# Attention: earlier places for the odd head's score tiles, and other places for values, maxima and decoding

## The chip, the cores and the metric

The kernel runs on one core of a Trainium2 chip. A core has TensorE (PE in the profile; its weight loads are shown apart as PEld), VectorE (DVE), ScalarE (ACT), GpSimd (POOL) and SyncE (SP, which issues most transfers). The metric is device time of one execution in microseconds. Three runs of the kernel before gave 985.89 us in the median, 984.61 at the lowest and 988.9 at the highest.

## The reference, cut to what matters

Attention with a threshold on each row of scores, and then two feed-forward layers on its output. The change touches the attention alone: 4 batches of 8 heads, 576 positions, 64 columns a head.

```python
scale = 1.0 / np.sqrt(q.shape[-1])
scores = scale * np.matmul(q, k.transpose(0, 1, 3, 2))
thresh = np.max(scores, axis=-1, keepdims=True) - tau
scores = np.where(scores >= thresh, scores, -1000000000.0)
scores = scores - np.max(scores, axis=-1, keepdims=True)
attn = np.exp(scores)
attn = attn / (np.sum(attn, axis=-1, keepdims=True) + 1e-09)
return np.matmul(attn, v).astype(np.float32)
```

The weights of the two layers arrive as 64-bit floats; the kernel decodes them to 32 bits itself.

## The kernel before

**Pairs and units.** The 32 heads are worked off as 16 pairs, an even and an odd head each. A pair is nine units, numbered through as u = 9 p + n. One unit takes a tile of 128 keys of a head against all 576 queries: n = 0 to 3 are tiles of the even head, n = 4 holds the last 64 keys of both heads (so it has twice the matmuls), n = 5 to 8 are tiles of the odd head.

**What is done in a unit.** For the pair at hand: `shifted` forms a tile `zt` of scores with the row shift already subtracted (four matmuls of 288 columns, eight in unit 4), `expo` takes its exponent on ScalarE, `mask` zeroes on VectorE what lies under the threshold, `p_split` splits the result into a high part `phi` (ScalarE) and a low part `plo` (GpSimd), and three units later `values` multiplies with the values of the head: three steps of two matmuls (`phi` with the high part of v, `phi` with the low part, `plo` with the high part). For the next pair, inside the same units: `transpose_kq`, `split_kq` (a cast on ScalarE, `lo` on VectorE), the stacking transfers `stack_k` and `stack_q` on SP's queue (among them `q_st<-lo`), the plain score tiles `scores` (`sc`, four matmuls, five tiles a head), `row_max` on VectorE for each of them, and from the five maxima of a head `row_shift`, `shift_turn` and `shift_store` (the last with a transfer that ScalarE issues). `store_head` copies a finished head from PSUM with ScalarE (`xs`) and sends it off through SP.

**What sets the order.** All engines get their work in program order; nothing is rearranged later. ORDER (line 68) has one string for each unit of a pair, and `attention_unit` (line 690) walks through it. E is the shifted tile and its exponent, v one values step and V all that are left, S a score tile, x a maximum, M the mask, p the split of the unit before, F, P, A, T and L run the lists of splits, transposes, row shifts and v splits, transfers and head stores that are due in that unit, J makes one step of weight decoding. A letter whose list is empty in a unit does nothing.

**Score tiles.** S_UNITS (line 63) says in which unit, counted from the first unit of a pair, each of the ten score tiles of that pair is issued: five entries of the even head, then five of the odd head. All lie in the pair before.

**Weight decoding.** Eight blocks of the first layers' weights are decoded under the attention, at most two at a time. A block is a generator that yields, after each step, how many J it must wait and of which kind the next step is ("a", "s", "b", or any). DECODE (line 92) says which kinds are taken at the J of each unit. The steps of a block: load; absolute value (ScalarE, L489, kind a); clamp (VectorE, L491, s); shift (VectorE, L494, s); combine (VectorE, L497, b); exponent (VectorE, L501, s); scale (VectorE, L504, b); add (GpSimd, L508, any); cast (ScalarE, L535, any); difference (GpSimd, L537, any). What is left at the end of the attention is run off before the first layer goes on.

**PSUM.** `tr` (transposes), `sc` and `zt` come from one pool of three buffers of two banks each (`ps_r`), and the tile in which the values of a head are summed from another with one buffer (`ps_av`).

Of the kernel before, what the change touches and what calls it, by code (L numbers as in the profile page):

```python
# [21 lines left out]
def kernel(  # L22
# [37 lines left out]
    DELTA = 2.0 ** -22  # L60
    U0 = -18
    T_A, T_B = -16, -10
    S_UNITS = (-10, -9, -7, -7, -6, -5, -4, -3, -3, -2)
    TURN_AT = 4
    JOB_EVERY = 14


    ORDER = (
        "FESvSxvMxxpVPLTASJ",
        "vFEvSSTSxxMxxxpLVPAJ",  # L70
        "EvvvSSSMxxxVLFPATpJ",
        "FESvSSxxMxxpVLPATJ",
        "FESSSMJvxxxpVLPAT",
        "FEvvSSSMxxxpVLPATJ",
        "FvJEvSSSMxxxpVLPAT",
        "FEvvvSSSMxxxVLPvATpJ",
        "FSEvPSSTMxxxpVLAJ",
    )
    STACK = (1, 3)
# [9 lines left out]
    X_EARLY = 6  # L89
    X_FIRST = 4  # L90
    IN_EARLY = (0, 2)
    DECODE = ('', '', 's', 'asb', '', 's', '', 'as', 'asb')
    ON_PE = (0, NT // P - 1)
    LAGO = 2
    CL = 2
# [550 lines left out]
    def at(d, u, f, *args):  # L646
        d.setdefault(max(u, U0), []).append((f, args))
# [29 lines left out]
    for p in range(NP):  # L677
        for n, d in enumerate(S_UNITS):
            at(s_at, UNITS * p + d, None, 2 * p + n // NTI, n % NTI)
        for j in range(2):  # L680
            t = UNITS * p + S_UNITS[NTI * j + NTI - 1]
            at(act_, t + 1, row_shift, 2 * p + j)
# [7 lines left out]
    def attention_unit(u):  # L690
# [9 lines left out]
        for what in ORDER[u % UNITS]:  # L700
# [22 lines left out]
            elif what == "J" and u >= JOBS_FROM:  # L723
                jobs.step("asb" if u < 0 else DECODE[u % UNITS])

# [401 lines left out]
```

## Time and profile before

| | us |
|---|---|
| median of three runs | 985.89 |
| profiled execution | 985.73 |
| its span, first to last instruction | 983.9 |
| thirteen pairs, 50.69 to 338.34 | 287.65 |
| rest of the kernel, 376 to 984 | 608.0 |

The profiled execution's own time is 1.8 us longer than its span. The pairs of the attention follow each other up to about 372 us; what comes behind, the two layers, the change does not touch, apart from the last weight block. The granted clock of TensorE is 1.00 in each stretch of the windows view, the upper of its two levels (2.4 GHz). A row of the timeline with "x2" is two instructions of one kind in a row; a value in brackets is how long the engine had been idle before it and what ended the wait.

### The profile page before, as it was taken

To read this page: it belongs to the slowest core of one execution; us is meant where nothing else is said; L and a number is where in the kernel's file an instruction comes from. 1 tells how busy PE (TensorE), PEld (TensorE's weight loads), DVE (VectorE), ACT (ScalarE), POOL (GpSimd) and SP (SyncE) were. 2 spreads that over 40 slices of the span, in tenths; PEclk is the share of its full clock that TensorE was granted. 3 is DMA by queue.
4 is the path that set the end of the run, shared out by engine and by line. 5 is a ranking of instruction groups with operands and counts; after the bars stand their busy time and mean duration, and the time that the engine had idled before them with its cause. 6 is when DMAs were issued, how large, how long until landed. Compare 5 with 4: busy or idle time off the path is not lost.

```text
span 983.9 us, 15050 instructions
## 1 busy us (share of the span) xinstructions
PE 953.3 (97%) x5232; PEld 839.6 (85%) x5232; DVE 711.5 (72%) x1128; ACT 494.6 (50%) x926; POOL 603.0 (61%) x573
## 2 busy tenths in 40 slices
PE   4999999999999999999999999999999999999998
PEld 3899988998899988889988998899889988888886
DVE  2788788878778755788767886788775686666561
ACT  2576776776676676454333333333334434434433
POOL 6477877987898788668545643564457704433422
PEclk9999999999999999999999999999999999999999
DMA  6565566666655513221221222111301214434453
GB/s 159 123 138 142 122 134 168 143 164 157 150 137 125 126 50 73 64 77 65 76 74 54 65 65 75 65 65 65 118 31 48 61 43 122 136 108 128 109 143 92
DMA packets 89885, 99.89 MB, mean 102 GB/s; under 512 B 50032, under 2 KB 62640, under 8 KB 89808
## 3 DMA queue, kind: packets, MB, share of 16 engines
q1 hardware_dynamic: 89424, 98.76, 38.9%
q8 instruction: 41, 0.67, 0.3%
q14 instruction: 36, 0.29, 0.1%
q10 hardware_dynamic: 384, 0.16, 0.1%
HBM read 55.13 MB, written 15.88 MB: 72 GB/s over the span
## 4 chain that ended last, share of the span: by engine, by line
PE 77%; DVE 7%; ACT 5%; issue 3%; POOL 2%; SPq 2%; DMA 2%; ACTq 1%; DVEq 0%; POOLq 0%
PE y L801 20%; PE h L763 19%; PE o L956 10%; PE h L845 10%; PE av L430 7%; PE zt L380 6%; PE sc L303 4%; DVE e L398 3%; ACT e L393 2%; DVE mcol L316 2%; ACT phi L406 1%; DVE lo L269 1%; PE tr L260 1%; ACT xs L442 1%; DVE raw L501 1%
## 5 line engine op out<-in xcount | busy, mean ns | idle before, releaser
L407 POOL TENSOR_TENSOR plo<-e,phi 128x576 fp32r<-128x576 f32 x144 | 206.6, 1444 | 54.2 <-ACT phi L406 53.7
L784 POOL TENSOR_TENSOR gl<-cl,gh 128x512 fp32r<-128x512 f32 (+1 forms) x80 | 100.4, 1255 | 167.9 <-ACT gh L783 91.7
L801 PE MATMUL y<-gh,wg 128*128 128x512 f32 (+1 forms) x640 | 186.8, 373 | 0.0
L763 PE MATMUL h<-xh,wg 128*128 128x512 f32 (+1 forms) x640 | 184.2, 369 | 0.7 <-DVE e L398 0.7
L398 DVE SCALAR_TENSOR_TENSOR e<-zt,ntau,e 128x576 f32<-128x576 f32 x144 | 117.0, 813 | 63.5 <-ACT e L393 47.3
L801 PEld LDWEIGHTS y<-gh,wg 128*128 128x128 f32 x640 | 118.8, 188 | 17.1
L763 PEld LDWEIGHTS h<-xh,wg 128*128 128x128 f32 x640 | 118.4, 188 | 17.4 <-DVE e L398 1.0
L393 ACT ACTIVATE e<-zt 128x576 f32<-128x576 f32 x144 | 93.6, 650 | 74.7 <-PE zt L380 52.1
L801 PE MATMUL y<-gl,wg 128*128 128x512 f32 (+1 forms) x320 | 120.1, 375 | 0.5 <-POOL gl L784 0.4
L316 DVE TENSOR_REDUCE mcol<-sc 128x1 f32<-128x576 f32 x160 | 117.2, 748 | 3.8 <-PE sc L303 3.6
L763 PE MATMUL h<-xl,wg 128*128 128x512 f32 (+1 forms) x320 | 118.0, 369 | 0.0
L780 ACT ACTIVATE cl<-cl,half 128x512 f32<-128x512 f32 (+1 forms) x80 | 54.4, 680 | 98.5 <-DVE cl L779 98.4
L783 ACT CAST gh<-cl 128x512 fp32r<-128x512 f32 (+1 forms) x80 | 46.3, 578 | 112.5 <-DVE cl L782 106.7
L956 PE MATMUL o<-wg,ln 128*128 128x512 f32 x432 | 102.4, 393 | 0.0
L845 PE MATMUL h<-wg,y 128*128 128x512 f32 x432 | 101.2, 390 | 0.0
L406 ACT CAST phi<-e 128x576 fp32r<-128x576 f32 x144 | 96.3, 669 | 1.5 <-DVE e L398 0.9
L956 PEld LDWEIGHTS o<-wg,ln 128*128 128x128 f32 x432 | 80.9, 188 | 18.4 <-ACT ln L919 0.2
L845 PEld LDWEIGHTS h<-wg,y 128*128 128x128 f32 x432 | 81.0, 188 | 16.8
L920 POOL TENSOR_TENSOR ln<-land,ln 128x1024 fp32r<-128x1024 f32 x16 | 38.5, 2405 | 92.4 <-ACT ln L919 92.4
L779 DVE TENSOR_SCALAR cl<-h 128x512 f32<-128x512 f32 (+1 forms) x80 | 50.6, 632 | 55.1 <-PE h L763 51.3
L380 PE MATMUL zt<-q_st,k_both 128*128 128x288 f32 x320 | 75.1, 316 | 5.1 <-DVE lo L269 3.8
L303 PE MATMUL sc<-k_both,q_st 128*128 128x288 f32 x320 | 72.7, 310 | 5.4 <-DMA q_st<-lo 3.9
(110 smaller groups left out, 1874.9 us busy)
## 6 DMA issues: line engine op xcount, KB each, us to landing
raw<-in_moe_w_in_dram SPq DMA_DIRECT2D x24, 512.0 KB
raw<-in_moe_w_out_dram SPq DMA_DIRECT2D x24, 512.0 KB
k_both<-q_st SPq DMA_DIRECT2D x30, 288.0 KB
sq<-so SPq DMA_DIRECT2D x64, 128.0 KB
land<-sq SPq DMA_DIRECT2D x16, 512.0 KB
k_both<-lo SPq DMA_DIRECT2D x32, 144.0 KB
q_st<-lo SPq DMA_DIRECT2D x32, 144.0 KB
x<-xs SPq DMA_DIRECT2D x32, 144.0 KB
```

Of the source, the lines that this page charges most:

```text
L303: nc.tensor.matmul(ps[:, c, 0:HS], lhsT=st[j][i][r, n * P : n * P + P], rhs=kk[j][i][r, o + c * HS : o + (c + 1) * HS], start=(st is q_st) ...
L316: nc.vector.tensor_reduce(mc[:, n : n + 1], sc_ps.pop((h, n))[:, :, 0:HS], axis=AXES.XY, op=ALU.max, negate=True)
L380: nc.tensor.matmul(ps[:, c, 0:HS], lhsT=st, rhs=mv[:, c * HS : (c + 1) * HS], start=(m == 0), stop=(m == len(todo) - 1),)
L393: nc.scalar.activation(out=e, in_=st_ps[u][:, :, 0:HS], func=ACTF.Exp)
L398: nc.vector.scalar_tensor_tensor(out=e, in0=st_ps.pop(u)[:, :, 0:HS], scalar=ntau[:, 0:1], in1=e, op0=ALU.is_ge, op1=ALU.mult)
L406: nc.scalar.copy(hi, e)
L407: (nc.vector if u - NU in LO_DVE or u < NU - UNITS and u % UNITS in LO_UNITS else nc.gpsimd).tensor_tensor(lo, e, f32(hi), op=ALU.subtract)
L763: nc.tensor.matmul(ps, lhsT=a[:, kk, f], rhs=m[:, kk, :], start=(n == 0 and kk == 0), stop=(n == 2 and kk == KD - 1),)
L784: nc.gpsimd.tensor_tensor(gl, cl, f32(gh), op=ALU.subtract)
L801: nc.tensor.matmul(y_ps[c][d], lhsT=a[:, jj, ds_], rhs=m, start=(jj == 0 and n == 0), stop=(jj == JG - 1 and n == 2),)
L845: nc.tensor.matmul(ps[g], lhsT=a[:, kk, :], rhs=wg_t["in2", g][s][:, kk, :], start=(n < 2), stop=(n >= 6 * KD - 2),)
L956: nc.tensor.matmul(ps, lhsT=a[:, f, :], rhs=wg_t["out2", f // 4][m][:, f % 4, :], start=(n == 0), stop=(n == len(terms) - 1))
```

## The change

S_UNITS: the second and third score tile of the odd head are issued one unit earlier, so the odd head's five tiles are issued in units 4, 4, 5, 6, 7 of the pair before instead of 4, 5, 6, 6, 7. In the strings of units 2 and 7 one S comes before the third v. In unit 1 an x is moved behind V and L before it; in unit 3 A comes before P. DECODE: unit 8 no longer takes steps of kind b.

```diff
-    S_UNITS = (-10, -9, -7, -7, -6, -5, -4, -3, -3, -2)
+    S_UNITS = (-10, -9, -7, -7, -6, -5, -5, -4, -3, -2)
...
     ORDER = (
         "FESvSxvMxxpVPLTASJ",
-        "vFEvSSTSxxMxxxpLVPAJ",
-        "EvvvSSSMxxxVLFPATpJ",
-        "FESvSSxxMxxpVLPATJ",
+        "vFEvSSTSxxMxxpLVxPAJ",
+        "EvvSvSSMxxxVLFPATpJ",
+        "FESvSSxxMxxpVLAPTJ",
         "FESSSMJvxxxpVLPAT",
         "FEvvSSSMxxxpVLPATJ",
         "FvJEvSSSMxxxpVLPAT",
-        "FEvvvSSSMxxxVLPvATpJ",
+        "FEvvSvSSMxxxVLPvATpJ",
         "FSEvPSSTMxxxpVLAJ",
     )
...
-    DECODE = ('', '', 's', 'asb', '', 's', '', 'as', 'asb')
+    DECODE = ('', '', 's', 'asb', '', 's', '', 'as', 'as')
```

## Rows read from the trace of the kernel before

**Rows 1.** The page, busy time of each engine.

```profile
span 983.9 us, 15050 instructions
...
PE 953.3 (97%) x5232; PEld 839.6 (85%) x5232; DVE 711.5 (72%) x1128; ACT 494.6 (50%) x926; POOL 603.0 (61%) x573
```

**Rows 2.** Windows view: us, busy time of each engine (instructions), clock, DMA.

```profile
317.12:338.34 21.22, 21.17 (x154) 19.98 (x153) 16.01 (x24) 14.87 (x30) 16.54 (x18) 1.00 0.51 119
...
50.69:338.34 287.65, 280.98 (x1978) 260.20 (x1977) 234.34 (x318) 201.89 (x393) 234.58 (x233) 1.00 0.61 142
```

**Rows 3.** Waits of the weight loads, 50 to 357 us: total, times, longest.

```profile
PEld zt L380 <- DVE lo L269: 7.5, 16, 0.9
PEld zt L380 <- DVE e L398: 4.7, 18, 0.3
...
PEld av L430 <- POOL plo L407: 4.0, 11, 0.7
```

**Rows 4.** Two lines of decoding, 29 to 383 us: ns min/median/max.

```profile
L501 DVE TENSOR_SCALAR raw<-dec_a x8: 448/1455/1621, 57.8 to 302.2; 128x512 uint32<-128x512 uint32 x8
...
L497 DVE SCALAR_TENSOR_TENSOR dec_a<-raw,dec_a x8: 674/1419/1459, 50.7 to 294.9; 128x512 uint32<-128x512 uint32 x8
```

**Rows 5.** Timeline, units 2 to 4 of a pair with decoding: start, us.

```profile
231.01 0.42 PE L380 MATMUL zt<-q_st,k_both 128*128 128x288 f32 x2
...
234.67 1.43 POOL L407 TENSOR_TENSOR plo<-e,phi 128x576 fp32r<-128x576 f32 x1 [1.22 <-ACT phi L406]
...
234.79 1.60 DVE L501 TENSOR_SCALAR raw<-dec_a 128x512 uint32<-128x512 uint32 x1
...
237.16 0.53 PE L380 MATMUL zt<-q_st,k_both 128*128 128x288 f32 x2 [0.64 <-DVE lo L269]
...
238.34 0.43 PE L303 MATMUL sc<-k_both,q_st 128*128 128x288 f32 x2
```

**Rows 6.** Timeline, units 2 to 4 of the pair from 317.12.

```profile
320.31 0.42 PE L380 MATMUL zt<-q_st,k_both 128*128 128x288 f32 x2
...
321.49 0.44 PE L430 MATMUL av<-plo,v_hi 128*128 128x288 f32 x2
...
321.76 0.43 PE L303 MATMUL sc<-k_both,q_st 128*128 128x288 f32 x2
...
321.97 0.62 ACTq L347 DMA_DIRECT2D q_m<-mt  x1
...
322.68 0.64 ACT L442 COPY xs<-av 128x576 f32<-128x576 f32 x1 [0.74 <-PE sc L303]
...
326.77 0.50 PE L303 MATMUL sc<-k_both,q_st 128*128 128x288 f32 x2
...
327.68 0.82 DVE L398 SCALAR_TENSOR_TENSOR e<-zt,ntau,e 128x576 f32<-128x576 f32 x1 [0.90 <-ACT e L393]
```

**Rows 7.** Timeline, units 6 and 7 of the pair from 227.62.

```profile
241.78 0.43 PE L380 MATMUL zt<-q_st,k_both 128*128 128x288 f32 x2
...
243.27 0.82 DVE L398 SCALAR_TENSOR_TENSOR e<-zt,ntau,e 128x576 f32<-128x576 f32 x1 [0.34 <-ACT e L393]
...
244.14 0.53 PE L380 MATMUL zt<-q_st,k_both 128*128 128x288 f32 x2
```

**Rows 8.** End of the stage in the timeline; below it the lines view, 30:380.

```profile
383.55 1.30 POOL L784 TENSOR_TENSOR gl<-cl,gh 128x512 fp32r<-128x512 f32 x1 [3.94 <-ACT gh L783]
...
L508 POOL TENSOR_TENSOR dec_a<-dec_a,raw 128x512 f32<-128x512 f32 x8 | 10.5, 1314 | 5.4 <-DVE raw L504 5.4
```

**Rows 9.** Timeline, first score tile of unit 4 in two other pairs.

```profile
128.31 0.50 PE L303 MATMUL sc<-k_both,q_st 128*128 128x288 f32 x2 [0.57 <-DMA v_nat<-in_v_dram]
...
345.42 0.59 SPq L291 DMA_DIRECT2D q_st<-lo  x1
...
347.99 0.50 PE L303 MATMUL sc<-k_both,q_st 128*128 128x288 f32 x2 [0.56 <-DMA q_st<-lo]
```

## Prediction

> **What bounds the kernel now.** I read the page first: TensorE is busy 953.3 of 983.9 us [rows 1], and it stays the engine in whose order everything waits. The change touches only the attention stage, so I cut that stage by pairs of heads (one pair is nine units) with the windows view. Thirteen pairs, from 50.69 to 338.34, take 287.65 us, 22.13 each; the shortest, from 317.12, takes 21.22 [rows 2]. While that shortest pair runs no weight block is being decoded, so about 0.9 us per pair is lost to something that comes and goes. Busy time does not show it (21.17 of 21.22 us there [rows 2]), because matmul records overlap: two matmuls of 288 columns follow each other every 0.27 us although each pair of them is listed as 0.43 [rows 6]. So I went to the waits of the weight loads, between 50 and 357 us [rows 3]. Three matter: a shifted score tile `zt` waits for VectorE's `lo` (7.5 us, 16 times), for VectorE's mask (4.7 us, 18 times), and a values matmul `av` waits for GpSimd's `plo` (4.0 us, 11 times). Then I looked at each place in the timeline.
>
> **How the three PSUM buffers rotate.** All `tr`, `sc` and `zt` tiles share three buffers, and walking through the program, handing out the buffer that is released first, tells who waits for whom. Before: `zt` of unit 4 takes the buffer that `lo` releases, `zt` of unit 7 that of unit 6's mask, because two `sc` tiles stand between them. After: `zt` of unit 7 takes the buffer of unit 5's maximum, which is long free, but `zt` of unit 5 takes that of unit 4's mask.
>
> **The change part by part.**
>
> *Nothing at all:* the strings of units 1 and 3. Unit 1 has no score tile, so its x is empty, and unit 3 has no P and no A work.
>
> *Decoding leaves units 2 and 8 (DECODE).* I walked the eight weight blocks through the step list. A block has two steps that are marked "b". Before, units 3 and 8 of a pair take such a step, and all eight blocks are done by unit 115; after, only unit 3 does, a block takes two pairs, and the eighth ends at unit 148. Before, unit 2 does a decode step of VectorE or a cast of ScalarE in 12 pairs; after, in one (unit 20). The steps land in units 3 (16 times), 5, 7 and 8. What this is worth: in the pair at 227.62 the step of L501 in unit 2 starts at 234.79 and lasts 1.60 us, VectorE's `lo` stands behind it, and `zt` of unit 4 waits for `lo` until 237.16. From unit 2's `zt` (231.01) to unit 4's first `sc` (238.34) it is 7.33 us [rows 5]; in the pair without decoding 326.77 - 320.31 = 6.46 [rows 6]. Of the 14 pairs from 50.69 to 357 the excess over 6.45 sums to 9.1 us. Not all of it comes back. The first `sc` of unit 4 needs the transfer `q_st<-lo`: where TensorE came early it waited for that transfer until 347.99, 2.57 us after its issue [rows 9]. In one pair that `sc` starts only at 128.31, 8.1 us after its unit 2, under another wait for a transfer [rows 9], and 1.4 us of it stays; the pair with the step of unit 20 keeps its 0.9; I take 0.4 off for small lateness of the transfer elsewhere. 9.1 - 1.4 - 0.9 - 0.4 = 6.4 us gained. Bounds: 0 (the transfer or `xs` takes over each time) and 8.
>
> The same kind of step has two prices: L501 takes 0.448 at least and 1.455 in the median, L497 0.674 and 1.419 [rows 4]; the long ones lie under a running GpSimd `plo` (234.67 for 1.43 us, over the 1.60 us step) [rows 5]. The Trainium skill, "SBUF — State Buffer", section "Who interferes with whom", says that VectorE and GpSimd share one port pair as an exclusive lock, so such a step blocks until the GpSimd instruction ends; the trace agrees, the step ended at 236.39, 0.29 us after `plo`. By that rule a step that meets a `plo` in unit 3 waits as well, and the time would be that of rival 2.
>
> Unit 8 keeps seven steps where it had eleven, in front of `lo` of unit 0, for which `zt` of unit 1 waits today (a share of the 7.5 us). I take 0.4 us gained, bounds -0.7 and 1.5.
>
> *Odd score tiles one unit earlier (S_UNITS).* No matmul is added or removed; 4 x 0.133 us move from unit 6 to unit 4 (and unit 5 exchanges one tile for another). Gained: in unit 7 `zt` starts at 244.14, 2.36 us after unit 6's, against 16 matmuls x 0.133 (half of 0.27) = 2.13; it waits for the mask that ends at 243.27 + 0.82 = 244.09, and its first two matmuls then take 0.53 instead of 0.43 [rows 7]. That is 0.23 + 0.10 = 0.33 us per pair. Paid: in unit 5 `zt` will wait for unit 4's mask. In the pair without decoding that mask ends at 327.68 + 0.82 = 328.50, while TensorE would come there at 326.77 + 14 x 0.133 = 328.63, its weight load 0.13 sooner [rows 6]: a wait of about 0.05, with a restart of 0.1. A decode step of unit 3 now always stands in front of that mask; there VectorE is idle 0.90 us today, waiting for ScalarE's exponent [rows 6], and the short price (L497: 0.674) fits in, the long one (1.419) passes it by 0.52 [rows 4]. I take 0.2 us per pair; bounds 0 and 0.7. Fifteen pairs: 15 x (0.33 - 0.20) = 2.0 us, bounds -5.5 and 5. The second `sc` of unit 4 waits for unit 3's mask, which ends before it is due by some 0.2 us; the maxima are behind masks as before, so they cost nothing while VectorE has its gaps (234.34 of 287.65 us busy [rows 2]).
>
> *Third values step behind the first `sc` in units 2 and 7.* It uses `plo`, and comes 4 x 0.133 = 0.53 us later. Ten of the 11 waits for `plo` [rows 3] are in these two units, and nine of the ten are shorter than 0.53. Those of unit 2 are already in the 9.1 us; of the others I count 1.0 us, bounds 0 and 1.6. Queued behind that values step is ScalarE's copy `xs`, then SP's `sums`, `x` and `q_st<-lo`. Today `xs` starts at 322.68, held not by TensorE but by ScalarE's own issue of `q_m` (321.97 + 0.62 = 322.59); the moved step would start at 321.49 + 0.53 = 322.02 and end near 322.45 [rows 6]. So I cost it at nothing; without that cover it is 0.5 us per pair (first rival).
>
> *The end of the stage.* The last block's addition, cast and difference now fall after the last `plo`. GpSimd stood idle 3.94 us there [rows 8]; two instructions of 1.3 us [rows 8] fit. The cast delays ScalarE's chain by about 0.5 us, which TensorE's queue mostly covers: I take -0.4 us, bounds -1.5 and 0. Nothing changes after that, and nothing in the start-up, where TensorE's order of the moved tiles is the same.
>
> *Sum:* 6.4 + 0.4 + 2.0 + 1.0 - 0.4 = 9.4 us. The profiled execution took 985.73 us (span 983.9), 0.16 under the median of the runs, 985.89. 985.73 - 9.4 = 976.3; I say 976.5. As a cross-check, the clean pair of 21.22 with 0.13 off, times 13, is 274.2 against 287.65; so the sum leaves some 4 us of what is lost today in place.
>
> **The rivals.**
>
> 1. *`xs` follows the moved values step.* If ScalarE sees the step's end 0.5 us later than its own issue allows, `q_st<-lo` goes out 0.5 us later and unit 4's `sc` waits. Then clean pairs lose 0.5 and decoded ones gain only 0.4: the 6.4 falls to about 0.5. For it: where TensorE came early, `sc` did stand waiting for that transfer [rows 9]. Against: the 0.2 us between 322.45 and 322.68. Time: 976.3 + 5.9 = 982.2.
>
> The Trainium skill, "DMA: Bandwidth & Descriptors", section "Anatomy of one DMA", gives about 2.0 us fixed plus size over 436 GB/s: an estimate of 2.34 us for these 64 x 576 x 4 bytes; the trace has 2.57 from issue to use [rows 9], and by both the transfer does not shorten when TensorE gets faster.
>
> 2. *The step in unit 3 takes its long price* (under a running `plo`): the mask of unit 4 is late by the 0.52 us above, 15 times 7.8 us, of which 0.05 x 15 was counted. Time: 976.3 + 7 = 983.3. For it: the medians of L497 and L501 [rows 4]. Against: the long ones I found stood in units 2 and 8, the short ones after units 3 and 5.
>
> 3. *Slower: VectorE becomes the pace of units 3 to 5.* Two maxima, two masks, `lo` and a decode step now stand between the `zt` of unit 4 and of unit 5, and TensorE's queue stands still behind `zt` of unit 5. It decides from the point where that wait passes the gains: 9.4 + 15 x 0.2 = 12.4 us over 15 pairs, 0.83 us each. If the wait were as long as a long step, 1.4 us each: 15 x 1.4 = 21 less 12.4, so 8.6 slower, 994. Against: VectorE's idle 0.90 us in front of that mask [rows 6].
>
> 4. *Same:* the wait for `lo` is not the decoding's but ScalarE's cast in front of `lo`, and the waits that go come back one unit later at the masks: the 6.4 and the 2.0 fall away, 985.73 - 1.0 = 984.7.
>
> **How the numbers follow.** Forecast as summed 0.62 (971 to 981), rival 1 0.11, rival 2 0.10, rival 4 0.10, rival 3 0.07. Half a per cent is 4.9 us, about what a measurement can tell from no change. Faster: the forecast and the better half of rivals 1 and 2, 0.73; same 0.20; slower 0.07. The range reaches down to 970 (the gaining bounds of all terms together, 8 + 1.5 + 5 + 1.6 = 16) and up to 983.5 (rivals 1 and 2).
>
> **What would show it.** In the profile after: the pairs take about 21.4 us each; the wait of `zt` for `lo` falls from 7.5 to under 2.5 us; unit 7's `zt` waits for no mask, but unit 5's does, 0.05 to 0.2 us each; waits for `plo` fall under 1 us; `xs` in unit 2 starts still about 2.4 us after the unit's `zt`. The forecast is wrong if unit 4's `sc` begins later than 6.6 us after unit 2's `zt`, or if the mask of unit 4 ends more than 3.3 us after unit 4's `zt`.

## The result and the profile after

977.27 us in the median (976.56 to 977.83, four runs) against 985.25 for the kernel before beside it: ratio 0.9914, 95% interval 0.9889 to 0.9939. The change makes the kernel 0.9% faster; 976.5 was forecast. The profiled execution took 977.77 us with a span of 976.0, so 7.96 less than before's.

First the page of the kernel after, then its windows: thirteen pairs, the last of them alone, pair 7 and pair 15 (both to be explained), and below them pair 15 of the kernel before. Pairs are numbered from 0 at the stage's start; pair 15 runs from its first `zt` to its last.

```profile
span 976.0 us, 15048 instructions
...
PE 946.7 (97%) x5232; PEld 839.1 (86%) x5232; DVE 712.2 (73%) x1128; ACT 497.1 (51%) x926; POOL 602.2 (62%) x573
```

```profile
50.26:328.42 278.16, 273.47 (x1978) 259.75 (x1977) 229.34 (x314) 202.53 (x391) 226.72 (x229) 1.00 0.63 147
307.48:328.42 20.94, 20.94 (x154) 20.00 (x153) 17.70 (x28) 15.60 (x31) 16.79 (x18) 1.00 0.59 148
178.73:201.00 22.27, 21.20 (x155) 19.97 (x153) 17.83 (x26) 15.65 (x31) 18.68 (x20) 1.00 0.68 170
348.72:363.30 14.58, 12.91 (x88) 11.13 (x86) 8.91 (x10) 10.74 (x21) 14.43 (x14) 1.00 0.20 58
```

```profile
358.75:371.31 12.56, 11.78 (x87) 11.20 (x86) 6.68 (x8) 10.29 (x21) 12.36 (x13) 1.00 0.23 67
```

Thirteen pairs take 278.16 us, 21.40 each, against 22.13 [rows 2]. The pair from 307.48, with decoding, now takes less than the shortest pair did before, which had none (20.94 against 21.22). But pair 7 lasts 22.27, and the last pair is 2.0 us longer than it was.

The waits of the weight loads after, 50 to 348 us, and below them two lines of decoding, 29 to 383 us:

```profile
PEld sc L303 <- DVE e L398: 3.5, 7, 1.1
PEld sc L303 <- issue: 2.2, 2, 1.3
...
PEld sc L303 <- DVE raw L504: 1.2, 1, 1.2
PEld av L430 <- POOL plo L407: 0.9, 5, 0.2
PEld zt L380 <- DVE lo L269: 0.9, 1, 0.9
PEld zt L380 <- DVE e L398: 0.8, 5, 0.2
```

```profile
L501 DVE TENSOR_SCALAR raw<-dec_a x8: 420/644/1456, 64.8 to 360.7; 128x512 uint32<-128x512 uint32 x8
L497 DVE SCALAR_TENSOR_TENSOR dec_a<-raw,dec_a x8: 1151/1166/1428, 59.8 to 357.2; 128x512 uint32<-128x512 uint32 x8
```

Against [rows 3], the wait of `zt` for `lo` fell from 7.5 to 0.9, for the mask from 4.7 to 0.8, of `av` for `plo` from 4.0 to 0.9. The waits of `sc` grew from 2.1 us (1.3 behind VectorE's mask, 0.8 "issue") to 6.9 in these three rows. Of the 6.9 us, 5.2 stand in unit 4: there the view names VectorE or "issue", but in the longer ones the engine named had long been done and the transfer `q_st<-lo` landed last (below). The other 1.7 stand in unit 7.

Where it went, place by place. Sums over pairs 1 to 14, worked out from the starts of `zt` and `sc` in the timeline of each kernel; "first sc" is the first score tile of unit 4. The last columns are pair 15 and the whole stage, first to last `zt`:

| us | zt 0 to zt 2 | zt 2 to zt 4 | zt 4 to first sc | first sc to zt 6 | unit 6 | unit 7 | unit 8 | pair 15 | stage |
|---|---|---|---|---|---|---|---|---|---|
| before | 47.64 | 81.64 | 17.80 | 48.58 | 32.96 | 37.70 | 41.75 | 12.56 | 341.71 |
| after | 45.03 | 75.01 | 20.12 | 57.13 | 22.34 | 37.54 | 41.29 | 14.58 | 333.83 |
| DECODE alone | 44.68 | 76.15 | 18.02 | 48.74 | 32.98 | 40.18 | 41.31 | 14.41 | 337.56 |
| after, v back | 44.66 | 75.94 | 17.48 | 57.52 | 22.33 | 40.04 | 40.90 | 14.76 | 334.42 |
| after, S_UNITS back | 44.69 | 74.96 | 19.52 | 49.20 | 32.98 | 37.79 | 41.67 | 14.40 | 336.26 |
| after, DECODE back | 47.78 | 81.56 | 16.85 | 56.83 | 22.35 | 36.44 | 42.19 | 12.55 | 337.51 |
| before, no step in unit 2 | 47.46 | 77.93 | 17.60 | 48.68 | 34.22 | 37.96 | 41.89 | 12.56 | 339.38 |

The moved score tile is 14 x 4 x 0.133 = 7.45 us that leaves unit 6 and enters the column before it. Behind the stage's last `zt` each of these kernels has 612.5 to 612.7 us left, so nothing was won or lost there. The first `zt` comes at 27.8 to 29.6 us from execution to execution, which the stage column leaves out and the median does not. Each row is a single execution, so differences of a few tenths in it need not come from the edit: below, three pairs that an edit does not touch differ by 1.4 us together.

Now the places in the timeline. Units 2 to 5 of the pair from 307.48, the answer to [rows 6] and, since this pair now decodes, to [rows 5]; its last two rows are `zt` of units 6 and 7, which answer to [rows 7]:

```profile
310.67 0.42 PE L380 MATMUL zt<-q_st,k_both 128*128 128x288 f32 x2
...
313.04 0.64 ACT L442 COPY xs<-av 128x576 f32<-128x576 f32 x1 [0.74 <-DMA k_both<-lo]
...
314.56 0.55 SPq L291 DMA_DIRECT2D q_st<-lo  x1
...
316.00 0.43 PE L380 MATMUL zt<-q_st,k_both 128*128 128x288 f32 x2
...
316.23 1.43 POOL L407 TENSOR_TENSOR plo<-e,phi 128x576 fp32r<-128x576 f32 x1 [0.47 <-ACT phi L406]
...
317.05 1.16 DVE L497 SCALAR_TENSOR_TENSOR dec_a<-raw,dec_a 128x512 uint32<-128x512 uint32 x1
...
317.13 0.50 PE L303 MATMUL sc<-k_both,q_st 128*128 128x288 f32 x2
...
318.14 0.81 DVE L398 SCALAR_TENSOR_TENSOR e<-zt,ntau,e 128x576 f32<-128x576 f32 x1
...
319.06 0.47 PE L380 MATMUL zt<-q_st,k_both 128*128 128x288 f32 x2
...
321.22 0.43 PE L380 MATMUL zt<-q_st,k_both 128*128 128x288 f32 x2
...
322.82 0.43 PE L380 MATMUL zt<-q_st,k_both 128*128 128x288 f32 x2
```

`zt` of unit 4 follows unit 2's by 5.33 us and the first `sc` by 6.46: that is the clean pair's figure, with a decode step in unit 3. `xs` comes 2.37 us after `zt` (2.37 in [rows 6]), `q_st<-lo` goes out 3.89 after it. Unit 4's mask ends at 318.95, 2.95 after its `zt`, and unit 5's `zt` starts 1.93 after the `sc` where 14 x 0.133 = 1.86 would do. Unit 6 is 1.60 long, twelve matmuls at 0.133 without a wait.

Pair 7, where the new wait stands: SP's queue in pairs 6 and 7, `zt` and first `sc` of unit 4, and SP's own wait from 178 to 192 us:

```profile
178.62 1.18 SPq L469 DMA_DIRECT2D rb<-rec  x2
179.90 0.53 SPq L519 DMA_DIRECT2D raw<-in_moe_w_out_dram  x1
180.53 0.64 SPq L283 DMA_DIRECT2D k_both<-q_st  x1
...
187.32 0.46 SPq L291 DMA_DIRECT2D q_st<-lo  x1
...
187.46 0.43 PE L380 MATMUL zt<-q_st,k_both 128*128 128x288 f32 x2
...
189.76 0.50 PE L303 MATMUL sc<-k_both,q_st 128*128 128x288 f32 x2 [1.07 <-issue]
```

```profile
SPq L291 <- DMA k_both<-q_st: 1.3, 1, 1.3
```

An rb load and a raw block are issued right behind each other, the stacking transfer `k_both<-q_st` behind them lands late, `q_st<-lo` waits 1.3 us for it and goes out 5.20 us after unit 2's `zt` (182.12) instead of 3.89, and the `sc` comes 7.64 after it. The new DECODE has its raw loads in unit 7 of pairs 4, 6, 8, 10 and 12; the rb loads (one every six units) fall in that unit in pairs 6 and 10, and pairs 7 and 11 wait.

The end of the stage, GpSimd from pair 14 on, and TensorE's wait in pair 15 (the answer to [rows 8]); the last row is the wait from 338 to 376 us, which was 0.4 us in the kernel before:

```profile
338.73 1.31 POOL L508 TENSOR_TENSOR dec_a<-dec_a,raw 128x512 f32<-128x512 f32 x1 [0.63 <-DVE raw L504]
...
341.39 1.58 POOL L251 TENSOR_TENSOR v_lo<-v_nat,v_hi 128x640 fp32r<-128x640 f32 x1
...
345.00 1.44 POOL L477 TENSOR_TENSOR x<-x,rb 128x576 f32<-128x576 f32 x1
...
349.16 1.32 POOL L537 TENSOR_TENSOR wg<-dec_a,wg 128x512 fp32r<-128x512 f32 x1
...
351.91 0.30 PEld L430 LDWEIGHTS av<-plo,v_hi 128*128 128x128 f32 x2 [0.93 <-POOL plo L407]
```

```profile
PEld av L430 <- POOL plo L407: 3.2, 7, 0.9
```

The addition and the difference of the last but one block fall in pair 14, with `v_lo` and a normalisation; from 338.73 on GpSimd has no gap over 0.1 us left and runs behind to the end of the pair.

### The profile page after: what moved, and what is told of

It is laid out like the page before. It is cut to its first block, busy times and chain, and to the rows that moved or that the text cites. A ratio compares the mean times of both kernels' runs of the same rounds, so it can differ in the third digit from the quotient of the medians.

```text
span 976.0 us, 15048 instructions
## 1 busy us (share of the span) xinstructions
PE 946.7 (97%) x5232; PEld 839.1 (86%) x5232; DVE 712.2 (73%) x1128; ACT 497.1 (51%) x926; POOL 602.2 (62%) x573
## 4 chain that ended last, share of the span: by engine, by line
PE 88%; POOL 4%; DVE 2%; issue 2%; SPq 2%; ACT 1%; DMA 0%; ACTq 0%; DVEq 0%; POOLq 0%
PE y L801 20%; PE h L763 20%; PE av L430 11%; PE o L956 10%; PE h L845 10%; PE sc L303 8%; PE zt L380 7%; PE tr L260 2%; POOL plo L407 2%; DVE e L398 1%; POOL wg L537 0%; ACT e L393 0%; POOL x L477 0%; DVE xl L740 0%; POOL xl L740 0%
## 5 line engine op out<-in xcount | busy, mean ns | idle before, releaser
L380 PE MATMUL zt<-q_st,k_both 128*128 128x288 f32 x320 | 71.8, 306 | 0.8 <-DVE lo L269 0.6
```

The costliest lines, as they stand in the source:

```text
L380: nc.tensor.matmul(ps[:, c, 0:HS], lhsT=st, rhs=mv[:, c * HS : (c + 1) * HS], start=(m == 0), stop=(m == len(todo) - 1),)
```

## The experiments

"Ratio" is to the kernel before, measured beside it on the same chip; medians of different kernels can come from different chips.

**The four parts alone and undone.** DECODE alone:

```diff
(before)
-    DECODE = ('', '', 's', 'asb', '', 's', '', 'as', 'asb')
+    DECODE = ('', '', 's', 'asb', '', 's', '', 'as', 'as')
```

> The kernel before with the new DECODE alone. My theory (the decode steps of unit 2 hold VectorE's lo, for which zt of unit 4 waits): the weight loads' wait of zt for lo falls from 7.5 to about 1 us, unit 2's zt to unit 4's first sc loses some 5 us over 14 pairs, and about 2 us come back as a loss in the last pair, where GpSimd has the last block's steps: 981 to 982.5 us, ratio to the kernel before 0.996 to 0.9975. The waits of zt for the mask in units 7 and of av for plo stay (4 to 5 us, 2.5 to 4 us). Rival (the transfer q_st<-lo takes the wait over at once, and the gain of the whole change is that of the moved score tiles and values steps): 984.5 to 986 us.

980.72 us, ratio 0.995 (0.993 to 0.9971): 4 to 5 us, a little more than expected. Its waits of the weight loads, 50 to 350 us:

```profile
PEld av L430 <- POOL plo L407: 5.1, 12, 0.6
...
PEld zt L380 <- DVE lo L269: 0.9, 1, 0.9
```

The first `sc` comes 81.64 + 17.80 - 76.15 - 18.02 = 5.3 us earlier, so the rival (the transfer takes the wait over) fails. Not expected: the first two units also gain 3.0, and unit 7 loses 2.5. There `av` waits 2.7 us for `plo` where it waited 1.0, and `sc` 1.0 in pair 1; with them the waits for `plo` come to 5.1 in all, where 2.5 to 4 were expected. Most of the 2.7 lies in pairs 6, 8, 10 and 12: there GpSimd works without a gap over 0.1 us from the addition in unit 4 on, through `v_lo`, the row shift and two `plo`, so `plo` does not gain what TensorE gained.

The third values step put back:

```diff
(after)
-        "EvvSvSSMxxxVLFPATpJ",
+        "EvvvSSSMxxxVLFPATpJ",
...
-        "FEvvSvSSMxxxVLPvATpJ",
+        "FEvvvSSSMxxxVLPvATpJ",
```

> The changed kernel with the third values step of units 2 and 7 back in front of the first S. My theory: that step waits for plo again, 1.0 us in all outside of what decoding did (0 to 1.6): 978.3 us, ratio to the kernel before 0.992 to 0.9935, waits of av for plo 1.5 to 3 us. Rival (the moved step decides how early the transfer q_st<-lo goes, since xs stands behind it): then this kernel is the faster one, 975 to 977 us, with the waits of sc in unit 4 gone.

977.85 us, ratio 0.9918 (0.9896 to 0.994): the time does not tell it from the change. In the trace:

```profile
PEld av L430 <- POOL plo L407: 6.2, 13, 0.8
...
PEld sc L303 <- DVE e L398: 2.5, 4, 1.0
```

The waits for `plo` are 5.3 us more (6.2 where 1.5 to 3 were expected), yet the stage is only 0.6 longer: unit 7 pays 2.5 and units 2 and 3 0.9, and the wait between `zt` 4 and the first `sc` gives 2.6 back (17.48 against 20.12). TensorE, held in unit 7 of pairs 6 and 10, no longer runs ahead of SP's queue in pairs 7 and 11: there `q_st<-lo` goes out at 3.89 and 3.86. That the later TensorE is the reason is argued: no run moves it alone. The rival (the moved step delays the transfer, since `xs` stands behind it) fails: in clean pairs the issue is at 3.86 to 3.89 in both kernels.

The old score tiles:

```diff
(after)
-    S_UNITS = (-10, -9, -7, -7, -6, -5, -5, -4, -3, -2)
+    S_UNITS = (-10, -9, -7, -7, -6, -5, -4, -3, -3, -2)
```

> The changed kernel with the old S_UNITS (odd score tiles in units 4, 5, 6, 6, 7). My theory: zt of unit 7 waits for unit 6's mask again, 0.33 us a pair, and zt of unit 5 no longer waits for unit 4's mask (0.05 to 0.2 us a pair): 2.0 us slower than the changed kernel, 979.3, ratio to the kernel before 0.993 to 0.9945; unit 7 starts 2.3 to 2.4 us after unit 6 in clean pairs, against 2.1 less 0.53 for the tile that left. Rival (what unit 7 gains unit 5 pays): 977 to 977.8, no difference.

981.54 us (977.87 to 985.27, twelve runs), ratio 0.9965 (0.9945 to 0.9984). The stage is 2.43 us longer than after's, as expected; the median says 4, but its runs scatter over 7 us, so I take the trace for the size.

The old decoding:

```diff
(after)
-    DECODE = ('', '', 's', 'asb', '', 's', '', 'as', 'as')
+    DECODE = ('', '', 's', 'asb', '', 's', '', 'as', 'asb')
```

> The changed kernel with the old DECODE. My theory: the wait of zt for lo is back at 6 to 8 us, pairs with decoding take 7.0 to 7.4 us from unit 2's zt to unit 4's first sc, and the last pair gets back 2 us: 980.5 to 982.5 us, ratio to the kernel before 0.995 to 0.9975. Rival (decoding in unit 2 is not what cost the time, the other two parts carry it): 977 to 978.5 us.

979.79 us, ratio 0.9943 (0.9922 to 0.9964). Its first row of waits:

```profile
PEld zt L380 <- DVE lo L269: 9.0, 15, 0.9
```

The wait for `lo` is back, above the 6 to 8 expected, and pair 15 is at 12.55 again. So S_UNITS and the moved v are worth 4.2 us without the new decoding (341.71 - 337.51), more than the 3 that I had for them, and DECODE 3.7 on top.

**What in unit 2 costs.** Only VectorE's steps leave it; ScalarE's casts stay:

```diff
(before)
-    DECODE = ('', '', 's', 'asb', '', 's', '', 'as', 'asb')
+    DECODE = ('', '', '', 'asb', '', 's', '', 'as', 'asb')
```

> The kernel before with VectorE's decode steps kept out of unit 2 only; ScalarE's cast of each block still falls in unit 2 (8 times), and all blocks are done by unit 120. My theory (VectorE's step in front of lo is the larger part, the cast in front of ScalarE's own part of the split costs some 0.37 us each): the wait of zt for lo falls from 7.5 to about 3 us, time 4 us less, 980.5 to 982 us, ratio 0.9955 to 0.997. Rival (the cast is what holds lo): the wait stays over 6 us, 984 to 986 us.

982.66 us, ratio 0.9981 (0.9962 to 0.9999), half of the gain expected. The wait for `lo` fell about as expected:

```profile
PEld zt L380 <- DVE lo L269: 3.6, 15, 0.4
```

7.5 to 3.6, but these waits stand in two places. At `zt` of unit 4, which the edit is about, they fall from 6.4 to 1.8 us; at `zt` of unit 1 they rise from 1.0 to 1.8. So VectorE's step was over two thirds of the wait in unit 4, and what is left, 0.2 to 0.4 us in five of the eight pairs with a cast in unit 2, is the most that the cast can have. zt 2 to the first `sc` gains 3.9. But 1.3 us of it come back in unit 6 (34.22 against 32.96): more steps now stand in unit 5, in front of the masks. And one single step, the last that the changed kernel has in unit 2:

```diff
(after)
-    DECODE = ('', '', 's', 'asb', '', 's', '', 'as', 'as')
+    DECODE = ('', '', '', 'asb', '', 's', '', 'as', 'as')
```

> The changed kernel with unit 2's entry of DECODE empty, which moves one single VectorE step (unit 20) to unit 5 and nothing else. My theory of the price of such a step in unit 2: the one remaining wait of zt for lo (0.9 us, pair 2) goes, unit 2's zt to unit 4's first sc of that pair falls from 7.31 to 6.45, and the time by 0.8 us at most: 976.5 us, ratio to the kernel before 0.9905 to 0.992. Rival (that wait is of another cause than the step): it stays, 977.3 us.

975.81 us (974.3 to 976.99), ratio 0.9912 (0.9896 to 0.9928). Pair 2, 21.71 in the kernel after:

```profile
70.65:91.79 21.14, 21.11 (x154) 19.95 (x153) 17.82 (x25) 15.49 (x31) 16.68 (x18) 1.00 0.56 128
```

The wait for `lo` is gone, zt 2 to the first `sc` of pair 2 is 6.43 after 7.31. The interval doesn't tell the 0.9 us from the change; it is the lowest median of all kernels here. The stage of this execution is 2.2 us shorter (331.66), but 1.4 of that lies in pairs 4, 7 and 11, whose steps the edit leaves alone: so much differs from one execution to the next.

**SP's queue.** The rb loads one unit earlier:

```diff
(after)
-    NORM = (13, 6, 4)
+    NORM = (12, 6, 5)
```

> The changed kernel with the two rb loads of each normalisation issued one unit earlier (the normalisation itself stays where it is), so that they no longer stand in unit 7 beside the load of a raw weight block in pairs 6 and 10. My theory: that heap on SP's queue is why q_st<-lo goes out only 4.6 and 5.2 us after unit 2's zt in pairs 7 and 11 (3.9 elsewhere) and unit 4's sc waits: both go back to 3.9, pairs 7 and 11 fall from 22.27 and 21.89 to about 21.0, and the time by about 2 us: 975.3 us, ratio to the kernel before 0.989 to 0.9905. Rival (the raw block alone holds the queue): the late issue stays, 977.3 us.

978.89 us (974.04 to 982.8), ratio 0.9929 (0.99 to 0.9958): no faster. Yet pairs 7 and 11 did what was expected. SP's queue in pairs 6 and 7, then pair 7 (pair 11 is 21.28 too):

```profile
181.30 1.50 SPq L469 DMA_DIRECT2D rb<-rec  x2
...
183.90 0.54 SPq L519 DMA_DIRECT2D raw<-in_moe_w_out_dram  x1
...
190.49 0.55 SPq L291 DMA_DIRECT2D q_st<-lo  x1
```

```profile
183.25:204.53 21.28, 21.25 (x154) 20.02 (x153) 17.36 (x25) 15.65 (x31) 18.79 (x20) 1.00 0.68 173
```

`q_st<-lo` goes out 3.89 us after `zt` (186.60). What ate the 1.6 us is pair 4 of this execution, 24.14 against 22.05 (its first `zt` came late too, at 31.31 us). Three windows in a row:

```profile
127.00:128.30 1.30, 0.00 (x1) 0.04 (x1) 1.30 (x2) 1.30 (x3) 0.67 (x2) 1.00 0.60 184
128.30:130.40 2.10, 2.10 (x15) 2.10 (x16) 1.40 (x3) 0.77 (x3) 2.10 (x3) 0.92 0.68 141
130.40:132.00 1.60, 1.60 (x8) 1.59 (x8) 0.13 (x1) 0.34 (x1) 1.60 (x3) 0.50 0.93 213
```

TensorE stood 1.57 us in front of the first `sc`, and some 2 us later the granted clock fell from 1.00 to 0.50, the lower level: unit 5 took 3.52 us instead of 2.13. Both edits together:

```diff
(after)
-    DECODE = ('', '', 's', 'asb', '', 's', '', 'as', 'as')
+    DECODE = ('', '', '', 'asb', '', 's', '', 'as', 'as')
...
-    NORM = (13, 6, 4)
+    NORM = (12, 6, 5)
```

> The kernel of the run before (unit 2's entry empty) with the rb loads also one unit earlier. My theory: beside the 0.8 us of pair 2, pairs 7 and 11 fall from 22.27 and 21.89 to 21.3, 1.6 us: 975 us, ratio 0.989 to 0.9905; if a long wait of unit 4's sc in pair 4 takes TensorE's clock down in an execution, that execution is 2 us longer. Rival (moving the rb loads only moves the heap on SP's queue): 977 us or more.

976.44 us (975.35 to 982.03), ratio 0.9925 (0.9902 to 0.9947). Pair 11 fell to 21.19, but in pair 7 `q_st<-lo` went out at 4.74 and the pair took 22.33: moving the rb loads helps in pair 7 in one of the two executions seen. In this one the granted clock was 0.50 from 34.31 to 41.13 us, and pair 0 took 23.80 us against 20.80. No version, then, that is measurably faster than the change.

**The last pair.** Normalisations four units apart, so that one leaves pair 15:

```diff
(after)
-    NORM = (13, 6, 4)
+    NORM = (12, 4, 3)
```

> The changed kernel with the normalisations of a batch four units apart instead of six and their rb loads one unit earlier, so that one multiplication of GpSimd (1.4 us) leaves the last pair, and no rb load stands in the unit of a raw block's load. My theory: the last pair's 2 us are GpSimd's backlog (the addition and the difference of the next to last weight block in pair 14, 1.3 us each, with no gap behind them), so 1.4 us less work there brings 14.58 down to about 13.2; pairs 7 and 11 fall to 21.3; 974 to 975.5 us, ratio to the kernel before 0.9885 to 0.990. Rival (the last pair's wait is ScalarE's phi, not GpSimd's backlog; the multiplications only delay plo elsewhere): last pair 14 us or more, 977 us or more.

981.77 us, ratio 0.9973 (0.9959 to 0.9988): wrong. Pair 15 took 14.79. The last multiplication only went to its unit 0, still ahead of the `plo` that is late, so the run speaks neither for the backlog nor against it. And pair 7 took 26.78 us. SP's wait from 176 to 198 us, and two windows:

```profile
SPq L291 <- DMA k_both<-q_st: 3.9, 2, 2.7
```

```profile
188.00:190.00 2.00, 0.53 (x2) 0.30 (x2) 1.29 (x2) 1.25 (x3) 0.17 (x1) 1.00 0.49 121
190.00:192.00 2.00, 1.84 (x8) 1.87 (x9) 0.75 (x2) 0.99 (x3) 1.97 (x2) 0.50 0.68 175
```

How pair 7 came out in the kernels with a raw block there, from the transfers' issues and landings in each trace, in us from unit 2's `zt`:

| | raw block issued | `k_both<-q_st` landed | `q_st<-lo` issued |
|---|---|---|---|
| DECODE alone | -3.32 | 3.13 | 3.89 |
| after, v back | -3.30 | 3.61 | 3.89 |
| after, S_UNITS back | -2.76 | 4.43 | 4.50 |
| rb earlier | -2.69 | 3.27 | 3.89 |
| unit 2 emptied | -2.54 | 4.29 | 4.36 |
| both | -2.34 | 4.68 | 4.74 |
| after | -2.22 | 5.14 | 5.20 |

The later the 512 KB of the raw block are issued, the later lands the transfer behind them, with two exceptions (rb earlier and unit 2 emptied); where it lands at 4.29 or later, `q_st<-lo` waits for it. The issue of the block is not all: in pair 11 the transfer landed at 4.56 in the changed kernel and at 3.37 with v back, the block issued at -2.81 and -2.82. With four units between the normalisations the raw block went out at -0.56 and `k_both<-q_st` landed at 6.54.

Three other lists of DECODE end the decoding earlier:

```diff
(after, three kernels)
-    DECODE = ('', '', 's', 'asb', '', 's', '', 'as', 'as')
+    DECODE = ('', '', '', 'asb', '', 'sb', '', 'as', 'as')
...
+    DECODE = ('', '', '', 'asb', '', 's', '', 'asb', 'as')
...
+    DECODE = ('', '', '', 'sb', '', 'sb', '', 'asb', 's')
```

> The changed kernel with the list of DECODE empty in unit 2 and b taken in unit 5 as well: no step in unit 2 at all, casts in unit 6, additions in unit 4, all blocks done by unit 133 in place of 148. My theory (the 2 us lost in the last pair are GpSimd's part of the last block, and 0.9 us in pair 2 the step of unit 20): last pair 12.6 to 13.2 us to its last zt in place of 14.58, pair 2 some 0.8 less, less a few tenths for the longer steps in unit 5: 974.5 to 976 us, ratio 0.989 to 0.9905. Rival (two steps in unit 5 hold the masks there, GpSimd's addition in unit 4 holds plo): 977.5 us or more, with new waits of sc and av.

> The changed kernel with the list of DECODE empty in unit 2 and b taken in unit 7 as well: all blocks done by unit 119, casts in units 1 and 6, additions in units 4 and 8. By my theory the last two pairs are free of decoding: last pair 12.6 us in place of 14.58, pair 2 some 0.8 less: 974 to 975.5 us, ratio 0.9885 to 0.99. Rival (the steps only find other places to be in the way: GpSimd's addition in units 4 and 8 in front of plo, the cast of unit 1 in front of ScalarE's part of the split): 977 to 979 us, av waiting for plo over 3 us.

> The changed kernel with a list of DECODE that takes no step in unit 2, casts in unit 6, additions in unit 4, differences in unit 7, one VectorE step at most in a unit, and has all blocks done by unit 124. By my theory the last pair takes 12.6 us to its last zt instead of 14.58, pair 2 0.8 us less, pairs 7 and 11 (no raw load beside an rb load) 21.2; against it steps of L497 in units 5 and 7 that cost 0.1 to 0.3 us eight times: 974 to 976 us, ratio 0.9885 to 0.9905. Rival (each step moved out of units 2 and 3 into 5 and 7 costs as much there): 977.5 us or more.

978.53 us, 0.9922 (0.9898 to 0.9945); 979.25, 0.9937 (0.9916 to 0.9958); 979.59, 0.9955 (0.9939 to 0.997). None beats the change, against expectation three times. Pair 15 settles its own question. It took 14.13 us in the first, whose last addition and difference still fall in units 130 and 133 (pair 14), and 12.54 and 12.55 in the others, which end at 119 and 124. The second's:

```profile
352.13:364.67 12.54, 11.74 (x87) 11.19 (x86) 6.65 (x8) 10.26 (x21) 12.32 (x13) 1.00 0.25 67
```

All kernels with these two GpSimd steps in pair 14 have 14.1 to 14.8 there, all without 12.5 to 12.6. What the lists lose instead: the first and third wait more for `plo` in units 0 and 1 (47.53 and 50.12 us against 45.03), and in unit 7 (40.16 and 40.54 against 37.54) `sc` waits 2.9 and 3.4 us where it waited 1.7, and `av` 1.4 and 1.6 for `plo` where it waited 0.6; the second has ScalarE's cast in unit 1 of pairs 2, 5, 10 and 13, where unit 2 takes 3.9 to 4.1 us instead of 3.38.

## Why the prediction was right, point by point

The forecast case happened, and the sum was 9.4 us where 8.0 were measured. It held partly by luck, because errors of both signs met. By place the stage gave 4.3 (zt 2 to the first `sc`) + 2.6 (units 0 and 1) + 2.1 (first `sc` to unit 6) + 0.2 (unit 7) + 0.5 (unit 8) + 0.3 (pair 0) - 2.0 (pair 15) = 8.0 (7.9 by the stage column). And one of the prediction's own signs of being wrong came up: unit 4's `sc` begins later than 6.6 us after unit 2's `zt` in six of 14 pairs, 6.68 to 7.64 us after it, where only pairs 2 and 4 had been foreseen.

- *DECODE, unit 2, 6.4 us.* Mechanism right: `lo` is freed, 0.9 us of its wait is left, in the pair named. Size: 5.3 alone and 4.3 in the whole change. In the trace the waits for `lo` in unit 4 fall from 6.4 to 0.9 us and those for `plo` in unit 2 from 2.3 to nothing, but those of `sc` in unit 4 rise from 1.8 to 5.2. Of the 9.1 us of excess 4.8 stay, where the sum left 2.7: pairs 2 and 4 keep 0.9 and 1.2, about as counted, but pairs 7 and 11 keep 1.8 and pairs 9 and 14 another 0.9, for which I had 0.4 in all. In pairs 7 and 11 that is the load of raw blocks in unit 7, which I had not followed: I had walked the steps of a block to their units, but not its load through SP's queue. The fit behind the estimate of 2.34 us (the Trainium skill, "DMA: Bandwidth & Descriptors", section "Anatomy of one DMA") is stated there for transfers that GpSimd issues, and SP issues this one; in the second pair of [rows 9] it landed 2.44 us after its issue.
- *Unit 8, 0.4 us, at most 1.5.* Too small: units 0 and 1 gain 2.6, 3.0 with DECODE alone. This is the largest miss upwards, outside its bounds. The trace of the kernel before has 1.0 us of waits for `lo` at `zt` of unit 1, in six pairs, and 0.7 for `plo` in pair 10, behind GpSimd's difference and a normalisation; after, the former are gone, and 0.4 for `plo` is left in pairs 7 and 11.
- *S_UNITS, 2.0 us.* Measured 2.4 when undone. Inside it both halves were mis-sized: unit 6 gives (32.96 - 22.34 - 7.45) / 14 = 0.23 a pair, not 0.33 (the restart of 0.10 is not part of it), and unit 5 pays (57.13 - 48.58 - 7.45) / 14 = 0.08, not 0.20. Before the mask of unit 4 L497 had neither of its two prices: 1.166 in the median. The Trainium skill, "SBUF — State Buffer", section "Who interferes with whom", says that a VectorE instruction with two inputs in SBUF contends with a GpSimd one that reads there; the rows agree, L497 ends at 318.21, 0.55 us after the `plo` beside it (317.66). With that middle price rival 2 came true in small part: 0.08 us a pair where it had 0.52.
- *Third values step, 1.0 us.* 0.6, a balance: 3.4 gained in units 2, 3 and 7, 2.6 given back at the transfer. It is worth more than the plain count says, since it hides the waits for `plo` that the new decoding makes in unit 7, and less, since TensorE then reaches the transfer earlier.
- *End of the stage, -0.4, at least -1.5.* Wrong: -2.0, outside its bounds. Behind the last `zt` nothing changed, 612.6 and 612.7 us, as argued. But I looked only at the last block; the one before it adds in unit 130 and subtracts in unit 133, where GpSimd has no room.
- *Rivals.* `xs` did not follow the moved step (2.37 us after `zt` both times). VectorE did not become the pace of units 3 to 5. The half of rival 4 that says ScalarE's cast holds `lo` was true in small part: without VectorE's steps 1.8 of 6.4 us stayed in unit 4.

Left open: that units 0 and 1 gain because unit 8 has fewer steps is argued (no run moved those alone). So is why some executions of one kernel are 5 us longer than others: a fall of the clock stands in three of the profiles above, but with S_UNITS back two executions took 985.2 us at a mean granted clock of 1.00, and the timed runs show no timeline.

## What to carry to other kernels

Follow every instruction of a moved job through every queue, its load through SP and its GpSimd steps to the end of the stage, not only the step on the engine that is short of time: both of the larger losses here came from parts of the job that nobody was looking at. When a wait is removed, write down what is late next and by how much; a transfer with a fixed duration keeps what TensorE gains in front of it. And undo each part of a change singly: two edits that look independent paid for each other's waits.

## What the runs showed of the hardware

Single waits of 1.1 to 1.3 us of TensorE in unit 4 left the granted clock at 1.00 (pair 7 of the changed kernel above). One of 1.57 us was followed by 0.50, the lower level, some 2 us later, and two in one unit, of 0.83 and 1.52, by 0.50 for 6.8 us (the windows above). But the length of one wait does not settle it: with both edits the clock fell to 0.50 in pair 0, where TensorE had waited 0.71 us at most, and in the changed kernel it stayed at 1.00 there after a wait of 0.72. Where the clock falls, a stall costs more than its own length: after the wait of 1.57 us, 1.4 us more in one unit.

`q_st<-lo` lands 2.35 to 2.5 us after its issue in most pairs, but 3.1 to 4.0 in pair 4 of every kernel. In that stretch of the changed kernel (121.3 to 123.4 us) there is a packet of another queue:

```profile
q8 instruction: 1, 0.02, 3.7%
```

3.7% of 16 engines for 2.1 us are 1.2 us on one of them. Pair 9, the other late one, has such a packet too; pair 5, which is on time, has one of half the bytes in another queue (q14). In pairs 1 to 14 of all 14 kernels it is the same: the 28 transfers with a q8 packet that starts between 0.3 us before and 1.1 us after their issue, all in pairs 4 and 9, landed 2.85 to 4.01 us after it, the other 168 at most 2.84. That the loading of code delays the transfer is argued from this and not shown: no run moved such a packet.
